# A PSUM ring for scores and PV products, with a new step order, in a sliding-window attention and gMLP kernel

## The chip, the cores and the metric

The kernel runs on one core of a Trainium2 chip. The metric is the device time in microseconds of one execution. The profile and its trace come from one execution; its span is about 1.7 us shorter than that execution's time. Runs have a state: fast, or slow when a run is over 1.5% above the fastest of the same kernel. Ratios use fast runs alone; medians are of all runs of a call.

Engines in the profile: PE is TensorE, PEld its weight loads, DVE is VectorE, ACT is ScalarE, POOL is GpSimd, SP issues most DMAs. An instruction is named by its source line: L447 is line 447 of that kernel's file, so the same step has another line number in an edited kernel.

## The reference

Eight batches of 576 rows. Attention has 8 heads of 64 columns with a causal window of 64, and the layer behind it is a gated MLP with a spatial product:

```python
scores = scale * np.matmul(q, k.transpose(0, 1, 3, 2))
mask = (rel >= 0) & (rel < 64)                       # rel = row - column
attn = softmax(np.where(mask, scores, -1e9))
x = (attn @ v), heads side by side                   # B, 576, 512
h = np.maximum(x @ w_in, 0.0)                        # 512 -> 1024
u, v = h[..., :512], h[..., 512:]
v_n = (v - mean(v)) / np.sqrt(var(v) + 1e-6)
v_s = einsum('ts,bsd->btd', w_spatial, v_n) + b_spatial
return (u * v_s) @ w_out
```

## The kernel before

The kernel is one list of about 1200 short words. Each word is a step, and the words are issued in the order of the list; each engine then works through its own instructions strictly in that order.

```python
    for word in ORDER.split():
        op, *args = word.split(".")
        OPS[op](*[int(a) if a.isdigit() else a for a in args])
```

A batch `b` passes through these steps (`s` is a pair of heads; s = 4 holds the last 64 rows of all heads):

- `l`, `lv` load q, k, v on SP; `c`, `cv`, `sh` cast and shift them, mostly on GpSimd; `T` and `to` transpose.
- `S` scores on TensorE, `E` exp on ScalarE, `M` mask on VectorE, `P` the product with V and with ones on TensorE, `n1` ln of the row sums, `n2` exp(-ln) and `x` the product, which is the normalised attention.
- `V`, `U` the two halves of w_in, `Q` the rest rows; `vo`, `ru` evacuate them; `bs`, `rs`, `ln` are the norm (`rs` is an ln and an exp on ScalarE); `G`, `g` the spatial product, `O`, `oc`, `st` the output.
- `H` are warming matmuls on zeros; they are meant to keep TensorE's clock up.

Scores and PV products each have a buffer of two PSUM banks, everything else shares four single banks:

```python
    def mm(name, shape=(128, 512), dtype=f32):
        return new(psp, list(shape), dtype, "mm", 4, name)
    def pe_S(b, s):
        sc = new(psp, [128, 2, 512], f32, "sc", 1, f"sc{b}_{s}")     # one buffer
        ...
    def pe_P(b, s):
        oz = new(psp, [128, 2, 512], f32, "oz", 1, f"oz{b}_{s}")     # one buffer
        ...
```

`table` loads a table set for ScalarE that serves all of its functions:

```python
    _need = {AF.Exp, AF.Ln, AF.Copy, AF.Identity, AF.Relu}
    _tbl_id = next(i for i, (_n, _f) in enumerate(_tables.items()) if _need <= _f)

    def k_table():
        nc.scalar.add_instruction(
            mybir.InstLoadActFuncSet(name=f"I-{nc.next_id()}", act_func_set_id=_tbl_id,
                                     ins=[], outs=[]))
```

Nothing in the program depends on `table`: no tile is written by it and none is read.

The softmax here doesn't subtract the row's maximum and nothing guards it: scores larger than these inputs give would overflow.

Of the kernel before, what the change touches and what calls it, by code (L numbers as in the profile page):

```python
# [14 lines left out]
S = 576  # L15
# [5 lines left out]
keep scratch l.0.k.0 H.4 id mask lv.0.1 maskr lv.0.0 l.0.q.0 table l.0.q.1 H.6 l.0.k.1 c.0.k.0.D  # L21
l.0.q.4 l.0.q.2 cv.0.0.P l.0.k.2 lv.0.2 c.0.q.0.P H.2 l.0.k.4 sh.0.0.1.P T.0.q.0 l.0.k.3 T.0.k.0
to.0.q.0.A c.0.q.1.P to.0.k.0.D lv.0.3 ones.1 lv.0.5 c.0.k.1.D S.0.0 c.0.q.4.P l.1.q.0 T.0.q.1 E.0.0
small H.2 lv.0.4 H.3 c.0.q.2.P to.0.q.1.A M.0.0 sh.0.0.0.P lv.0.7 T.0.k.1 T.0.q.2 c.0.k.2.D l.0.q.3
P.0.0 lv.1.0 c.0.k.4.P n1.0.0 to.0.k.1.D T.0.k.2 n2.0.0 lv.0.6 S.0.1 x.0.0 l.1.k.0 cv.0.1.P H.4
E.0.1 to.0.k.2.D l.1.k.1 sh.0.1.1.P to.0.q.2.A sh.0.1.0.P lv.0.8 M.0.1 S.0.2 lv.1.1 cv.0.2.P
c.0.k.3.D E.0.2 P.0.1 l.1.q.1 win.1 H.3 n1.0.1 l.1.k.2 c.0.q.3.D T.0.k.3 sh.0.2.1.P n2.0.1 lv.1.3
to.0.k.3.D T.0.q.3 lv.1.2 H.2 to.0.q.3.A win.0 M.0.2 T.0.q.4 l.1.q.2 T.0.k.4 x.0.1 S.0.3 cv.0.3.P
E.0.3 sh.0.2.0.P P.0.2 l.1.q.3 n1.0.2 sh.0.3.1.P M.0.3 H.3 n2.0.2 sh.0.3.0.P to.0.q.4.A x.0.2 ones.0
wsp to.0.k.4.D P.0.3 n1.0.3 S.0.4 V.0.1.0.3 n2.0.3 lv.1.8 V.0.2.0.3 cv.0.4.P E.0.4 x.0.3 sh.0.4.0.P  # L30
V.0.0.0.3 M.0.4 V.0.1.3.4 c.1.k.0.P V.0.2.3.4 vo.0.1.D V.0.0.3.4 vo.0.2.A P.0.4 c.1.k.1.P n1.0.4
U.0.1 c.1.q.0.P n2.0.4 vo.0.0.A x.0.4 lv.1.4 cv.1.0.P U.0.0 bs.0.2 ru.0.1 bs.0.1 Q.0 ru.0.0 T.1.k.0
U.0.2 vo.0.4.A to.1.k.0.D T.1.q.0 bs.0.4 l.1.q.4 c.1.q.1.P V.0.3.0.3 to.1.q.0.A sh.1.0.0.P T.1.k.1
ru.0.2 S.1.0 to.1.k.1.D sh.1.0.1.P V.0.3.3.4 E.1.0 W.0 vo.0.3.D U.0.3 l.1.k.3 wo.0.A M.1.0 lv.1.5
T.1.q.1 W.2 bs.0.3 l.1.k.4 cv.1.1.P to.1.q.1.A P.1.0 ru.0.3 bs.0.0 sh.1.1.0.P W.4 lv.1.7 wo.2.A
S.1.1 c.1.q.2.P wo.4.D rs.0 W.1 lv.1.6 c.1.k.2.P U.0.4 ln.0.3 wo.1.A l.2.k.0 wout W.3 ln.0.0 ru.0.4
l.2.q.0 E.1.1 T.1.k.2 ln.0.2 T.1.q.2 ln.0.1 lv.2.5 wo.3.D to.1.q.2.A ln.0.4 G.0.1 l.2.q.3 M.1.1
n1.1.0 G.0.0 l.2.k.1 cv.1.2.P to.1.k.2.D n2.1.0 sh.1.2.0.P x.1.0 G.0.3 sh.1.1.1.P g.0.0 lv.2.2
c.1.q.3.P g.0.1 S.1.2 G.0.2 c.1.q.4.P E.1.2 g.0.3 c.1.k.4.P P.1.1 sh.1.2.1.P g.0.2 l.2.k.4 n1.1.1
O.0.0 c.1.k.3.P M.1.2 lv.2.1 n2.1.1 cv.1.3.P T.1.q.3 G.0.4 oc.0.0.A x.1.1 lv.2.0 to.1.q.3.A T.1.k.3  # L40
cv.1.4.P P.1.2 lv.2.4 to.1.k.3.D c.2.k.0.P n1.1.2 T.1.k.4 lv.2.3 g.0.4 T.1.q.4 S.1.3 sh.1.3.0.P
to.1.k.4.D n2.1.2 O.0.1 l.2.q.1 c.2.q.0.P E.1.3 x.1.2 O.0.2 sh.1.3.1.P lv.2.6 to.1.q.4.A M.1.3
c.2.k.1.P oc.0.1.A l.2.q.2 T.2.k.0 S.1.4 oc.0.2.A to.2.k.0.D lv.2.7 P.1.3 E.1.4 sh.1.4.0.P l.2.k.2
O.0.3 n1.1.3 M.1.4 c.2.k.4.P l.3.k.1 n2.1.3 T.2.q.0 V.1.1.0.2 l.2.q.4 to.2.q.0.A cv.2.0.P V.1.1.2.3
x.1.3 lv.3.0 V.1.0.0.2 oc.0.3.A sh.2.0.1.P V.1.0.2.3 P.1.4 st.0.1 cv.2.2.P S.2.0 n1.1.4 l.2.k.3
V.1.1.3.4 E.2.0 c.2.q.1.P V.1.2.0.2 vo.1.1.D V.1.3.0.2 cv.2.1.P l.3.k.3 n2.1.4 V.1.3.2.3 M.2.0
V.1.0.3.4 sh.2.0.0.P l.3.k.0 T.2.k.1 vo.1.0.A V.1.3.3.4 x.1.4 V.1.2.2.3 lv.3.3 vo.1.3.D V.1.2.3.4
c.2.q.2.P P.2.0 vo.1.2.A to.2.k.1.D lv.2.8 c.2.q.3.P T.2.q.1 n1.2.0 T.2.q.2 bs.1.1 U.1.0 l.3.q.3
sh.2.2.1.P n2.2.0 st.0.0 bs.1.3 cv.2.3.P to.2.q.1.A U.1.1 ru.1.0 lv.3.6 sh.2.1.0.P x.2.0 to.2.q.2.A
S.2.1 sh.2.3.1.P bs.1.2 lv.3.1 Q.1 E.2.1 c.2.k.2.P bs.1.0 lv.3.4 c.2.q.4.P ru.1.1 U.1.2 M.2.1  # L50
vo.1.4.A l.3.q.0 sh.2.1.1.P U.1.4 oc.0.4.A lv.3.7 bs.1.4 T.2.k.2 ru.1.2 U.1.3 l.3.q.2 c.2.k.3.P
ru.1.4 to.2.k.2.D rs.1 st.0.3 T.2.k.3 ru.1.3 ln.1.2 S.2.2 ln.1.1 P.2.1 l.4.k.2 E.2.2 ln.1.0 ln.1.3
T.2.q.3 lv.3.2 ln.1.4 G.1.0 c.3.q.3.P n1.2.1 M.2.2 l.3.k.2 n2.2.1 sh.2.2.0.P l.3.q.4 G.1.3
to.2.q.3.A x.2.1 l.4.k.4 to.2.k.3.D c.3.k.0.P P.2.2 l.3.q.1 cv.2.4.P g.1.0 n1.2.2 T.2.k.4 T.2.q.4
S.2.3 sh.2.3.0.P g.1.3 lv.4.1 n2.2.2 G.1.1 st.0.2 to.2.k.4.D c.3.k.1.P E.2.3 x.2.2 sh.2.4.0.P
l.3.k.4 G.1.4 g.1.1 to.2.q.4.A cv.3.3.P lv.3.5 T.3.k.1 M.2.3 G.1.2 cv.3.0.P st.0.4 to.3.k.1.D
l.4.k.5 S.2.4 P.2.3 sh.3.3.0.P g.1.2 l.4.k.6 n1.2.3 O.1.0 g.1.4 c.3.q.2.P c.3.q.0.P O.1.2 oc.1.0.A
c.3.q.4.P n2.2.3 st.1.0 T.3.k.0 c.3.k.2.P O.1.1 oc.1.2.A to.3.k.0.D l.4.q.2 sh.3.0.1.P E.2.4 l.4.q.0
x.2.3 T.3.q.0 c.3.q.1.P V.2.1.0.4 lv.4.2 to.3.q.0.A M.2.4 sh.3.0.0.P l.4.k.7 S.3.0 vo.2.1.A lv.3.8
P.2.4 oc.1.1.A c.3.k.3.P O.1.3 n1.2.4 cv.3.1.P E.3.0 V.2.2.0.4 sh.3.3.1.P oc.1.3.A T.3.q.1 M.3.0  # L60
sh.3.1.1.P V.2.3.0.4 n2.2.4 vo.2.2.A x.2.4 V.2.0.0.4 sh.3.1.0.P vo.2.3.A bs.2.2 cv.3.2.P Q.2
vo.2.0.A bs.2.1 c.3.k.4.P to.3.q.1.A bs.2.0 P.3.0 sh.3.2.1.P l.5.k.6 vo.2.4.A T.3.q.2 l.5.k.5
oc.1.4.A cv.4.1.P U.2.1 bs.2.4 l.5.q.7 n1.3.0 sh.3.2.0.P st.1.3 to.3.q.2.A bs.2.3 S.3.1 c.4.k.1.P
ru.2.1 T.3.k.2 l.4.k.1 U.2.0 to.3.k.2.D E.3.1 st.1.2 l.5.q.4 U.2.2 n2.3.0 M.3.1 l.4.q.3 ru.2.0
T.3.q.3 l.4.k.3 x.3.0 U.2.4 rs.2 l.4.q.5 T.3.k.3 ru.2.2 S.3.2 ln.2.1 l.4.q.1 ln.2.2 to.3.q.3.A P.3.1
l.4.k.0 ln.2.3 ru.2.4 U.2.3 ln.2.0 E.3.2 st.1.4 ln.2.4 lv.4.0 R.4.k.1 G.2.0 n1.3.1 l.5.q.3
to.3.k.3.D n2.3.1 l.4.q.6 G.2.1 M.3.2 ru.2.3 lv.4.3 x.3.1 S.3.3 g.2.0 l.5.q.0 P.3.2 E.3.3 g.2.1
c.4.q.0.P l.5.k.4 T.3.k.4 T.3.q.4 to.3.k.4.D G.2.3 to.3.q.4.A M.3.3 l.5.k.7 n1.3.2 c.4.k.0.P st.1.1
n2.3.2 G.2.4 g.2.3 G.2.2 l.5.q.6 x.3.2 cv.4.2.P g.2.4 l.4.q.7 P.3.3 cv.4.0.P g.2.2 l.6.k.2 n1.3.3
S.3.4 cv.3.4.P R.4.q.0 O.2.1 n2.3.3 sh.3.4.0.P R.4.k.0 l.4.q.4 O.2.2 oc.2.1.A sh.4.0.0.P x.3.3  # L70
V.3.0.0.4 oc.2.2.A sh.4.0.1.P E.3.4 O.2.0 vo.3.0.A M.3.4 cv.4.3.P V.3.3.0.4 bs.3.0 sh.4.1.0.P S.4.0
P.3.4 E.4.0 O.2.3 sh.4.1.1.P n1.3.4 M.4.0 V.3.1.0.4 oc.2.0.A c.5.k.1.P n2.3.4 st.2.0 V.3.2.0.4
vo.3.3.A x.3.4 l.5.k.0 vo.3.1.A bs.3.3 lv.5.0 P.4.0 c.4.q.1.P oc.2.3.A l.5.k.3 Q.3 bs.3.1 vo.3.2.A
l.5.q.5 n1.4.0 bs.3.2 lv.5.4 S.4.1 vo.3.4.A lv.5.1 U.3.0 R.4.q.1 E.4.1 l.5.q.2 bs.3.4 l.6.k.0 U.3.1
oc.2.4.A cv.5.0.P l.5.q.1 n2.4.0 U.3.3 lv.4.4 rs.3 x.4.0 l.5.k.2 ru.3.0 U.3.4 st.2.1 M.4.1 ru.3.1
S.4.2 l.5.k.1 ln.3.2 P.4.1 ln.3.4 E.4.2 ln.3.0 U.3.2 ln.3.1 st.2.2 ln.3.3 ru.3.3 M.4.2 G.3.0 lv.5.3
ru.3.4 n1.4.1 l.6.k.3 n2.4.1 S.4.3 g.3.0 ru.3.2 c.5.q.0.P G.3.1 x.4.1 E.4.3 cv.4.4.P P.4.2 g.3.1
lv.6.4 n1.4.2 G.3.2 M.4.3 lv.5.2 n2.4.2 l.7.q.3 c.5.k.0.P G.3.3 x.4.2 st.2.3 lv.6.1 g.3.2 cv.5.4.P
P.4.3 l.7.q.5 g.3.3 cv.5.3.P st.2.4 n1.4.3 S.4.4 R.5.q.0 G.3.4 sh.4.4.0.P E.4.4 l.6.k.1 O.3.0
R.5.k.0 n2.4.3 c.5.q.1.P M.4.4 O.3.1 cv.5.1.P l.6.q.4 O.3.2 g.3.4 oc.3.1.A l.7.k.4 x.4.3 cv.5.2.P  # L80
lv.6.2 S.5.0 oc.3.2.A R.5.k.1 lv.6.0 sh.5.0.1.P P.4.4 oc.3.0.A R.5.q.1 V.4.0.0.4 E.5.0 sh.5.1.1.P
l.6.k.6 V.4.3.0.4 vo.4.0.A lv.6.3 sh.5.1.0.P n1.4.4 bs.4.0 V.4.2.0.4 l.6.k.7 n2.4.4 vo.4.3.A l.6.q.5
x.4.4 V.4.1.0.4 sh.5.4.0.P M.5.0 l.6.q.2 cv.6.4.P O.3.3 vo.4.1.A l.6.q.0 vo.4.2.A bs.4.1 sh.5.0.0.P
S.5.1 Q.4 l.6.q.1 bs.4.2 E.5.1 c.6.k.0.P bs.4.3 P.5.0 oc.3.3.A l.6.q.7 vo.4.4.A S.5.2 cv.6.1.P
l.6.q.3 oc.3.4.A bs.4.4 U.4.0 n1.5.0 U.4.1 M.5.1 n2.5.0 lv.7.4 rs.4 x.5.0 st.3.1 U.4.2 E.5.2 ln.4.1
l.7.q.1 ln.4.2 U.4.3 ru.4.2 M.5.2 st.3.4 ru.4.0 P.5.1 ln.4.4 ru.4.1 ln.4.3 st.3.2 S.5.3 ln.4.0
n1.5.1 l.6.q.6 U.4.4 n2.5.1 G.4.0 ru.4.3 l.6.k.5 x.5.1 E.5.3 c.6.q.0.P lv.7.2 G.4.3 g.4.0 st.3.0
ru.4.4 M.5.3 cv.6.0.P P.5.2 l.6.k.4 g.4.3 n1.5.2 G.4.1 st.3.3 sh.6.0.0.P n2.5.2 G.4.2 x.5.2 cv.6.3.P
g.4.1 G.4.4 g.4.2 S.5.4 g.4.4 P.5.3 E.5.4 R.6.k.0 O.4.0 n1.5.3 cv.7.2.P M.5.4 c.6.q.1.P n2.5.3 O.4.2
R.6.q.0 O.4.1 x.5.3 oc.4.2.A cv.6.2.P oc.4.0.A R.6.q.1 st.4.2 V.5.1.0.4 sh.6.1.1.P l.7.k.6 V.5.0.0.4  # L90
l.7.k.5 vo.5.1.A c.6.k.1.P l.7.q.6 bs.5.1 P.5.4 vo.5.0.A l.7.k.1 S.6.0 oc.4.1.A l.7.q.2 bs.5.0
# [23 lines left out]
def kernel(  # L115
# [13 lines left out]
    f32 = dt.float32  # L129
# [37 lines left out]
    G = {}  # L167
# [509 lines left out]
```

## Time and profile before

| | before |
|---|---|
| time, median of 3 runs | 220.54 us (218.71 to 222.54) |
| profiled run | 227.03 us, span 225.3 us |
| TensorE busy | 206.5 us, 92% |
| ScalarE busy | 156.7 us, 70% |
| table loads on ScalarE | 2 |

A row of the timeline is: start, duration, engine, line, operation, output<-input, count; the bracket is the idle time ahead of it and what ended it. Two rows of ScalarE's timeline show how the softmax of batch 0 runs in the kernel before: the exp follows the ln at once.

```profile
11.77 0.60 ACT L493 ACTIVATE ln<-oz 128x512 f32<-128x512 f32 x1 [1.49 <-PE oz L487]
12.39 0.63 ACT L500 ACTIVATE zi<-ln 128x512 f32<-128x512 f32 x1
```

ScalarE had been idle for 1.49 us before this ln, because P was not done.

### The profile page before, as it was taken

What the parts mean: (1) busy time and instruction counts of PE and PEld (TensorE: products, weight loads), DVE (VectorE), ACT (ScalarE), POOL (GpSimd) and SP (SyncE); (2) the same over time, 40 slices, a digit from 0 to 9 for tenths busy, and PEclk for the clock granted to TensorE, in tenths of its full rate; (3) what the DMA queues carried; (4) which work ended last, traced back from release to release, by engine and by line L of the source; (5) the groups of instructions that cost most, each with busy time, mean ns of one, the idle gap of its engine ahead of it and who ended that gap; (6) DMA issues with size and microseconds to landing.
All of it is one profiled execution on the core that took longest, in us unless ns stands there. A gap on an engine that the chain in (4) does not pass through costs nothing.

```text
span 225.3 us, 6646 instructions
## 1 busy us (share of the span) xinstructions
PE 206.5 (92%) x2726; PEld 110.3 (49%) x2726; DVE 154.9 (69%) x299; ACT 156.7 (70%) x291; POOL 116.3 (52%) x162
## 2 busy tenths in 40 slices
PE   7866699899999899999999999998599999999993
PEld 2443236555555455555555545554454555454450
DVE  3466638987699938896787887584665968665530
ACT  6467357858797489965995779659367489857623
POOL 2769915998916996099313993067839700000000
PEclk9999679999999999999999999999769999999999
DMA  5999999999999869997499999999970014000605
GB/s 170 251 262 242 223 243 174 271 185 256 283 271 213 227 163 249 220 175 150 116 201 245 207 181 184 201 278 248 257 184 3 0 49 145 24 0 3 207 22 192
DMA packets 77647, 40.43 MB, mean 179 GB/s; under 512 B 44272, under 2 KB 73008, under 8 KB 77616
## 3 DMA queue, kind: packets, MB, share of 16 engines
q1 hardware_dynamic: 75392, 37.76, 73.7%
q0 software_dynamic: 2224, 2.24, 6.1%
q8 instruction: 21, 0.34, 0.7%
q14 instruction: 10, 0.08, 0.2%
HBM read 32.79 MB, written 9.44 MB: 187 GB/s over the span
## 4 chain that ended last, share of the span: by engine, by line
PE 55%; ACT 11%; DMA 10%; SPq 10%; POOL 6%; DVE 4%; issue 2%; POOLq 0%
PE ps L603 14%; PE pv L522 10%; PE po L617 9%; PE pu L580 8%; DMA win<-in_moe_w_in_dram 4%; DMA fk<-in_k_dram 4%; PE oz L477 4%; SPq L304 4%; PE oz L487 3%; PE sc L415 3%; DMA vf<-in_v_dram 2%; ACT ob L624 2%; SPq L295 2%; DVE vn L571 2%; DVE e L463 2%
## 5 line engine op out<-in xcount | busy, mean ns | idle before, releaser
L603 PE MATMUL ps<-wspT,vn 128*128 128x512 f16 (+1 forms) x256 | 39.0, 286 | 0.9 <-DVE vn L571 0.8
L508 DVE TENSOR_TENSOR x<-oz,zi 128x512 f16<-128x512 f32 (+1 forms) x40 | 25.2, 630 | 19.8 <-ACT zi L500 19.7
L493 ACT ACTIVATE ln<-oz 128x512 f32<-128x512 f32 (+1 forms) x40 | 22.4, 561 | 22.9 <-PE oz L487 22.6
L447 ACT ACTIVATE e<-sc 128x1024 f16<-128x1024 f32 x32 | 32.7, 1022 | 6.7 <-PE sc L404 4.6
L522 PE MATMUL pv<-win,x 128*128 128x512 f16 x128 | 33.3, 403 | 1.9 <-DMA win<-in_moe_w_in_dram 1.9
L580 PE MATMUL pu<-x,win 128*128 128x512 f16 x128 | 32.4, 395 | 0.0
L463 DVE TENSOR_TENSOR e<-e,mask 128x1024 f16<-128x1024 f16 x32 | 26.2, 820 | 8.4 <-ACT e L447 8.3
L617 PE MATMUL po<-wout,g 128*128 128x512 f16 x128 | 31.2, 380 | 0.0
L553 DVE BATCH_NORM_STATS2 st<-vs 128x6 f32<-128x512 f16 (+1 forms) x40 | 27.0, 674 | 4.9 <-ACT vs L547 4.8
L547 ACT ACTIVATE vs<-pv 128x512 f16<-128x512 f32 (+1 forms) x36 | 21.2, 601 | 11.5 <-PE pv L522 10.0
L610 DVE TENSOR_TENSOR g<-ps,ru 128x512 f16<-128x512 f32 (+1 forms) x40 | 24.2, 630 | 7.1 <-PE ps L603 6.8
L624 ACT COPY ob<-po 128x512 f32<-128x512 f32 (+1 forms) x33 | 18.8, 587 | 12.8 <-PE po L617 12.4
L500 ACT ACTIVATE zi<-ln 128x512 f32<-128x512 f32 (+1 forms) x40 | 23.6, 590 | 0.9
L603 PEld LDWEIGHTS <-vn 128*128 128x128 f16 x256 | 16.7, 97 | 14.8 <-DVE vn L571 2.0
L593 ACT ACTIVATE ru<-pu 128x512 f32<-128x512 f32 (+1 forms) x40 | 20.9, 553 | 2.1 <-PE pu L580 2.0
L354 POOL COPY vs<-vn 64x512 f16<-64x512 f16 (+1 forms) x24 | 21.1, 885 | 1.3
L331 POOL CAST nq<-fq 128x1152 f16<-128x1152 f32 x8 | 9.9, 1237 | 22.2 <-DMA fq<-in_q_dram 14.7
L340 POOL CAST vn<-vf 128x512 f16<-128x512 f32 (+1 forms) x24 | 15.6, 657 | 10.4 <-DMA vf<-in_v_dram 10.3
L522 PEld LDWEIGHTS <-x 128*128 128x128 f16 x128 | 12.6, 102 | 16.6 <-issue 4.7
L352 POOL COPY vs<-vn 64x512 f16<-64x512 f16 (+1 forms) x24 | 20.4, 848 | 0.5
L580 PEld LDWEIGHTS <-win 128*128 128x128 f16 x128 | 11.7, 100 | 13.5 <-issue 2.7
L603 PE MATMUL ps<-wspT,vlast 65*128 65x512 f16 (+1 forms) x64 | 17.1, 288 | 0.0
(102 smaller groups left out, 350.9 us busy)
## 6 DMA issues: line engine op xcount, KB each, us to landing
out_dram<-ob SPq DMA_DIRECT2D x32, 256.0 KB, 3.7
vf<-in_v_dram SPq DMA_DIRECT2D x40, 128.0 KB, 5.4
fk<-in_k_dram SPq DMA_DIRECT2D x32, 144.0 KB, 5.2
fq<-in_q_dram SPq DMA_DIRECT2D x32, 144.0 KB, 5.5
fk<-in_k_dram SPq DMA_DIRECT2D x16, 256.0 KB, 5.9
fq<-in_q_dram SPq DMA_DIRECT2D x16, 256.0 KB, 5.1
vf<-in_v_dram SPq DMA_DIRECT2D x16, 256.0 KB, 5.8
win<-in_moe_w_in_dram POOLq DMA_DIRECT2D x2, 512.0 KB, 10.0
```

The source lines that it names most:

```text
L447: nc.scalar.activation(e2[:, :, :], sc[0][:, :, :], AF.Exp, bias=0.0, scale=0.125)
L463: nc.vector.tensor_tensor(e2[:, :, :], e2[:, :, :], m, ALU.min)
L493: nc.scalar.activation(lnz[:, 0:n], OZ[b, s][:, 1, 0:n], AF.Ln)
L500: nc.scalar.activation(zinv[:, 0:n], lnz[:, 0:n], AF.Exp, bias=0.0, scale=-1.0)
L508: nc.vector.tensor_tensor(x[:, 0:n], oz[:, 0, 0:n], zinv[:, 0:n], ALU.mult)
L522: nc.tensor.matmul(PV[b, j][0:jn, :], xcol(b, r, j), w_in_sb[:, r, 512:1024], start=(r == 0), stop=(r == 3))
L553: nc.vector.bn_stats(st6[0:jn, 0:6], VSB[b, j][0:jn, :])
L580: nc.tensor.matmul(pu[:, :], w_in_sb[:, r, 128 * m:128 * m + 128], X[b, r][:, :], start=(r == 0), stop=(r == 3))
L603: nc.tensor.matmul(o, VN[b, kk][0:kn, 128 * mm_:128 * mm_ + 128], w, start=(kk == 0), stop=(kk == 4))
L610: nc.vector.tensor_tensor(g[:, :], ps[:, 0:n], RU.pop((b, m))[:, 0:n], ALU.mult)
L617: nc.tensor.matmul(po[:, :], G[b, r][:, 128 * j:128 * j + 128], w_out_sb[:, r, :], start=(r == 0), stop=(r == 3))
L624: COPY[e](ob[p, :], po[p, :])
```

## The change

Its intent: with a ring of two two-bank buffers, shared by scores and PV products in turn, S no longer waits for the E of the step before and P no longer for the x of the step before; and a search over step orders, on a timing model that was calibrated anew, gives the order that makes use of it. The code part is small:

```diff
-        sc = new(psp, [128, 2, 512], f32, "sc", 1, f"sc{b}_{s}")
+        sc = new(psp, [128, 2, 512], f32, "att", 2, f"sc{b}_{s}")
...
     def pe_P(b, s):
-        oz = new(psp, [128, 2, 512], f32, "oz", 1, f"oz{b}_{s}")
+        if s < 4:
+            oz = new(psp, [128, 2, 512], f32, "att", 2, f"oz{b}_{s}")
+        else:
+            oz = mm(f"oz{b}_4", (128, 2, 256))
```

The order is replaced as a whole, by the same words in another sequence. Two lines of it (the rest is cut):

```diff
-keep scratch l.0.k.0 H.4 id mask lv.0.1 maskr lv.0.0 l.0.q.0 table l.0.q.1 H.6 l.0.k.1 c.0.k.0.D
...
+G.0.4 cv.1.2.P g.0.1 to.1.q.2.A G.0.0 c.1.k.2.P g.0.4 table M.1.1 l.2.q.1 c.1.q.3.P T.1.k.2 T.1.k.3
```

## The prediction

> **What bounds the kernel now.** I read the page first: busy shares, then the 40 slices.
>
> ```profile
> PE 206.5 (92%) x2726; PEld 110.3 (49%) x2726; DVE 154.9 (69%) x299; ACT 156.7 (70%) x291; POOL 116.3 (52%) x162
> ...
> PE   7866699899999899999999999998599999999993
> ...
> PEclk9999679999999999999999999999769999999999
> DMA  5999999999999869997499999999970014000605
> ```
>
> TensorE is busy nearly everywhere except in the first five slices (28 us) and in slices 29 to 31, and in both places its clock drops. DMA is full until about 168 us and then nearly idle. This profiled run was a slow one: its span is 225.3 us and its time 227.03, against a median of 220.54, so a usual run has a span of about 219 (6 us less), and I must not explain those 6 us away as gain.
>
> Next the totals by stage (columns: stretch, its length, then busy us of PE, PEld, DVE, ACT, POOL, then granted clock, DMA share, GB/s).
>
> ```profile
> 0.00:25.58 25.58, 17.18 (x221) 9.35 (x222) 12.77 (x31) 16.70 (x26) 17.94 (x35) 0.97 1.07 232
> 25.58:31.30 5.72, 5.72 (x23) 2.01 (x23) 3.15 (x2) 0.60 (x1) 3.54 (x6) 0.52 1.21 201
> ...
> 49.34:157.60 108.26, 105.02 (x1543) 58.19 (x1541) 83.77 (x158) 85.74 (x161) 66.29 (x87) 1.00 0.98 214
> 157.60:168.50 10.90, 8.52 (x132) 5.15 (x132) 7.26 (x17) 5.62 (x11) 6.14 (x6) 0.69 1.03 230
> 168.50:221.50 53.00, 52.90 (x622) 26.35 (x612) 32.61 (x65) 34.70 (x70) 9.97 (x12) 1.00 0.17 59
> ```
>
> I turn this into a loss account. In dense stretches of the timeline a group of four 512-column matmuls takes 0.866 us, five take 1.08, an S step 0.35 (batches 0 to 3) or 0.59, a P step 0.60, a transpose step 0.225, a Q step 0.89. Summed over the step order this is 184 us of TensorE work, plus 6 us of warming matmuls. After the first O step (49.3 us) 158 us of it remain, and TensorE ends at 221.5: 172 us for 158, a loss of 14. Of that 5.4 lie in 157.6 to 168.5 (a wait of 2.3 us and then half clock, most likely this run's own), 1.6 after it, and some 7 in 49 to 157. Before 49.3 only 26 us of real work were done: that is where 23 us went, and it is the chain of waits that shows why:
>
> ```profile
> 10.46 4.97 DMA vf<-in_v_dram
> ...
> 15.50 0.67 POOL vs L352
> 16.16 0.51 POOL vn L337
> 16.68 8.86 DMA win<-in_moe_w_in_dram
> ...
> 25.58 5.28 PE pv L522 x12
> ```
>
> The first V product waits for w_in, whose load GpSimd issues only after twelve casts and shifts; the last x of batch 0 was ready at 25.46, at the same moment. So the start has two chains of equal length, w_in and the softmax chain of batch 0.
>
> **What the Trainium skill says.** "PSUM — Partial Sum Buffer", section "Specifications (TRN2)": eight banks of 512 fp32 values per partition. The kernel's buffers agree: sc 2 banks, oz 2, four single ones, 8 in all; the ring takes 2 x 2 plus 4, again 8. "TensorE: Matmul & The Clock Gate", Part 1: an idle window of about 3.4 us halves the clock, a busy one restores it. The trace agrees: clock 0.52 in 25.58 to 31.30. "ScalarE: Activation LUTs", sections "What ACT_TABLE_LOAD costs" and "Table sets: the hidden batching unit": about 1283 ns per load, plus a drain; `exp_and_others` has exp but not ln, `natural_log_exp_and_others` both; and a compiler pass puts a load before every activation that needs one. The before kernel shows two loads:
>
> ```profile
> 0.80 1.28 ACT L238 ACT_TABLE_LOAD   x1 [0.80 <-PEq L661]
> ...
> 3.47 1.28 ACT L205 ACT_TABLE_LOAD   x1
> 7.34 0.58 ACT L382 COPY tr<-tp_0q 128x512 f16<-128x512 f16 x1 [2.59 <-PE tp_0q L372]
> ```
>
> The duration agrees; the drain does not show (the copy before the second load ended at 3.45). L205 is the kernel's own step "table", which names a set with exp, ln, copy and relu. L238 is a load that nobody wrote: it was put ahead of the mask copy, because "maskr" stands before "table". So an activation reached before "table" gets a load of the compiler's choosing.
>
> **The change part by part.** I counted the words of both orders: the same 1173 steps with the same engine letters. No instruction is removed or added by hand; each row's duration should stay.
>
> 1. The ring. S(s+1) no longer waits for E(s), nor P(s+1) for x(s); instead each takes the older of two pairs of banks, and P of step 4 goes to the single buffers. What single buffers cost before: the waits put down to it are (who waited for whom: us in total, times, longest)
>
> ```profile
> ACT ln L493 <- PE oz L487: 22.6, 19, 3.4
> ...
> ACT e L447 <- PE sc L404: 4.6, 5, 2.6
> ...
> PE oz L477 <- DVE x L508: 2.0, 2, 1.3
> ```
>
> The last is the direct one: 2.0 us, two times, both in the first 23 us. ScalarE's 22.6 us before ln and 4.6 before exp are idle time of an engine that is not the bound. The ring can also give more overlap of E, M, P, n1, n2, x where TensorE waited on a mask step (0.41 us at 54.7, 1.11 at 77.6). I give the ring 1 to 3 us.
>
> 2. The order at the start. In the new order eleven, not twelve, casts and shifts precede w_in's load on GpSimd, and their inputs come earlier. Counting queue positions at 0.55 us each and about 4.5 us to landing, it should be issued near 14.5 instead of 16.7: w_in 2 us earlier.
>
> 3. Order and stores later. On the SP queue a store that waits holds the loads behind it: waits put down to L630 sum to 53.7 us in 12 times. One, from 102.3 to 109.0, is the dent of slices 18 and 19 of DMA. In the new order the comparable store of batch 2 stands even earlier (63 loads behind it, against 54), others later; no clear gain. Of the 8 us lost after 49 us in a usual run I let a better order recover 3.
>
> 4. "table" moves from before the first real activation to the middle of batch 1, after E.1.1. This is the part I weigh most. Until then ScalarE's order is exp, exp, ln, exp, ln, exp and so on. If the pass loads the exp set first and for each ln a set without exp, I count 14 loads: the mask copy, n1/n2 of steps 0 and 1 (4), n1.2, n2.2, n1.4, n2.3 (4), the two halves of rs.0, n1 and n2 of batch 1 step 0, and "table" itself. That is 12 more than now: 12 x 1.283 = 15.4 us of ScalarE, all before some 53 us.
>
> How much of it reaches the path? A load ahead of an ln can hide under the wait for P; one ahead of n2's exp cannot. Walking the steps with durations of the before profile (E 1.0, mask 0.7, P 0.6, ln 0.6, exp 0.63, to 0.58): with the loads, n1.0.0 falls at 14.5, n2.0.1 ends near 23, E.0.3 near 26, and from there four loads (5.1) and 2.8 us of activations lead to x.0.3 at about 34.7, against 25.5 now. Then V.0, U.0, the two loads of rs.0, and G.0 starts near 47.5 instead of 43.2; then T.1.k.3 needs a PSUM buffer that the evacuation of T.1.q.2 frees only behind two more loads and E.1.1, near 53. With 161 us of work left there, TensorE is some 7 us later than the before trace at the same point (161 left falls at 46).
>
> Sum with the loads: 220.5 + 7 (it contains the 2 us of w_in, which is then hidden) - 3 (ring and order later) = 224.5. Without them: 220.5 - 1.5 (start; the softmax chain of batch 0 binds then) - 3 = 216.
>
> **The rivals.** (a) The loads come and bind: 224.5. For it: the unwritten load at L238, and the fact that the kernel's author bothers to name one set. Against it: the search may know the loads. (b) The pass picks the common set at the first ln, or the loads hide: one or two more loads, 216. Nothing in the before trace shows how it picks. (c) The loads come but the lost time is regained, because DMA runs on while TensorE is late, and later waits for data (157 to 161 us) shrink: about 220. For it: DMA is full to 168 us and the chain runs through loads at 119 and 155. Against it: loads stand behind stores on SP, and these come later when TensorE is late. (d) The ring couples S to x two steps back, a longer chain than to E: S.0.4 would wait for x.0.1; 1 to 2 us worse, early only.
>
> **Range and chances.** I give the loads 0.8 (a and c together), and within them 224.5 and 220 some 2 to 1; (b) 0.2. An order that was searched would hardly have been kept had it been much worse on a chip, which pulls me below 224. The middle is 222.0 us, the range 214.5 to 228.5. Faster by over 2% is below 216.1: 0.16. Slower is above 224.95: 0.32. Within 2%: 0.52.
>
> **What would show it.** ACT_TABLE_LOAD in the groups: 14 and some 18 us for step 4 right, 2 or 3 for wrong. In the timeline, w_in issued near 14.5; x.0.3 near 35 (right) or 25 (wrong); the first 512-column G near 47. The 54 us before the end should stay dense as now. If DMA ends well before 160, my 3 us for the later order were too few. A prediction of 222 falls if loads are there and the time is still under 216: then the start was hidden under something that I took for following it.

## The result, and the profile after

| | before | after |
|---|---|---|
| time, median of 4 runs each | 221.54 us (218.71 to 223.41) | 228.66 us (226.99 to 229.41) |
| profiled span | 225.3 us | 227.7 us |
| mean granted TensorE clock in that run | 0.970 | 0.948 |
| TensorE busy | 206.5 us | 205.2 us |
| ScalarE busy, instructions | 156.7 us, 291 | 172.0 us, 303 |

The ratio is 1.0401, with a 95% interval of 1.0279 to 1.0523. Ratios here are the mean time of one kernel's fast runs over that of the other's fast runs of the same rounds, so they are not quite the ratio of the medians. The changed kernel is slower by 4%.

The slices of the changed kernel:

```profile
PE   7494575959899999999999999999999999999993
...
PEclk9957578897999999999999999999999999999999
```

The holes have moved. From slice 12 on TensorE is full and its clock is at 9 or more; the dip that the kernel before has in slices 28 to 30 is gone (its profile is of a slow run, so the dip may be that run's own). But the first eleven slices (63 us) are worse than before: TensorE at 4 to 5 tenths in five of them, and a clock under 9 in seven (3 to 8 and 10), where the kernel before had two such slices there, 5 and 6.

ScalarE's extra 15.3 us are twelve instructions. These are the table loads among the groups of the changed kernel (line, engine, operation, count, then busy us and mean ns of one, then idle time before):

```profile
L496 ACT ACT_TABLE_LOAD x5 | 6.4, 1283 | 0.1
L503 ACT ACT_TABLE_LOAD x5 | 6.4, 1283 | 0.1
...
L238 ACT ACT_TABLE_LOAD x1 | 1.3, 1283 | 0.8 <-PEq L664 0.8
L563 ACT ACT_TABLE_LOAD x1 | 1.3, 1283 | 0.0
L564 ACT ACT_TABLE_LOAD x1 | 1.3, 1283 | 0.0
L205 ACT ACT_TABLE_LOAD x1 | 1.3, 1283 | 0.0
```

L496 is n1, L503 is n2, L563 and L564 are the ln and the exp of `rs`. Fourteen loads, one at each change between exp and ln, until `table` (L205). ScalarE's timeline of batch 0, where before ln and exp stood next to each other:

```profile
13.93 1.02 ACT L447 ACTIVATE e<-sc 128x1024 f16<-128x1024 f32 x1 [0.94 <-PE sc L404]
14.97 1.28 ACT L496 ACT_TABLE_LOAD   x1
16.27 0.60 ACT L496 ACTIVATE ln<-oz 128x512 f32<-128x512 f32 x1
16.88 1.28 ACT L503 ACT_TABLE_LOAD   x1
18.18 0.63 ACT L503 ACTIVATE zi<-ln 128x512 f32<-128x512 f32 x1
...
20.82 1.28 ACT L496 ACT_TABLE_LOAD   x1
22.11 0.60 ACT L496 ACTIVATE ln<-oz 128x512 f32<-128x512 f32 x1
```

A load waits for no tile, so an empty bracket ahead of it does not tell whether it pushes the ln behind it. That is told by when P, for which the ln waits, was done on TensorE. P of step 0 ends at 15.20, so the load at 14.97 hides for only 0.2 of its 1.28 us; P of step 1 ends at 17.15, long before the load at 20.82, which does not hide at all. The load ahead of the third ln (28.50) does: the chain of waits passes there through matmuls of P that end at 29.81, and not through the load. The chain of waits of the changed kernel (start, us, what) runs through the same rows on to the first V product; a part of it:

```profile
32.35 0.04 ACT L496
32.38 1.26 issue
33.64 0.87 ACT ln L496 x2
34.51 0.02 issue
34.53 1.28 ACT L503
...
36.48 0.70 DVE x L511
37.19 0.05 issue
37.23 2.41 PE pv L525 x7
39.64 0.43 PE tp_0k L372 x4
40.07 1.61 PE pu L583 x4
```

Here a table load appears as "ACT L503" with no tile, or as "issue". Seven V products wait for the x at 36.48 and then take 2.41 us, where seven at full clock take 1.5 (7 x 0.2165 us, a fourth of a dense group of 0.866): TensorE has been waiting, and its clock is down. With the transposes and the U step behind them they take 4.45 us, where 2.6 would do (1.52, 0.22 and 0.87).

### The profile page after: what moved, and what is told of

It is laid out like the page before. It is cut to its first block, busy times and chain, and to the rows that moved or that the text cites. A ratio compares the mean times of both kernels' runs of the same rounds, so it can differ in the third digit from the quotient of the medians.

```text
span 227.7 us, 6658 instructions
## 1 busy us (share of the span) xinstructions
PE 205.2 (90%) x2726; PEld 109.6 (48%) x2726; DVE 151.4 (66%) x299; ACT 172.0 (76%) x303; POOL 113.0 (50%) x162
## 4 chain that ended last, share of the span: by engine, by line
PE 73%; ACT 15%; DVE 5%; issue 3%; DMA 2%; SPq 1%; POOL 0%; ACTq 0%
PE ps L606 14%; PE po L620 13%; PE pv L525 12%; PE pu L583 10%; PE oz L480 4%; PE oz L490 3%; PE pv L537 3%; PE sc L415 3%; PE sc L404 3%; ACT e L447 3%; ACT L503 2%; DMA fq<-in_q_dram 2%; DVE e L463 2%; ACT L496 2%; ACT zi L503 2%
## 5 line engine op out<-in xcount | busy, mean ns | idle before, releaser
L606 PE MATMUL ps<-wspT,vn 128*128 128x512 f16 (+1 forms) x256 | 39.6, 289 | 0.1
L525 PE MATMUL pv<-win,x 128*128 128x512 f16 x128 | 32.5, 387 | 3.8 <-DVE x L511 3.8
L496 ACT ACTIVATE ln<-oz 128x512 f32<-128x512 f32 (+1 forms) x40 | 21.8, 553 | 12.6 <-PE oz L490 12.2
L596 ACT ACTIVATE ru<-pu 128x512 f32<-128x512 f32 (+1 forms) x40 | 21.4, 552 | 8.0 <-PE pu L588 5.3
L503 ACT ACTIVATE zi<-ln 128x512 f32<-128x512 f32 (+1 forms) x40 | 23.4, 590 | 0.6
L354 POOL COPY vs<-vn 64x512 f16<-64x512 f16 (+1 forms) x24 | 18.9, 792 | 1.4
L525 PEld LDWEIGHTS <-x 128*128 128x128 f16 x128 | 11.4, 99 | 16.9 <-DVE x L511 5.2
L352 POOL COPY vs<-vn 64x512 f16<-64x512 f16 (+1 forms) x24 | 18.8, 782 | 0.7
L620 PEld LDWEIGHTS <-g 128*128 128x128 f16 x128 | 11.6, 98 | 12.9 <-DVE g L613 0.5
L583 PEld LDWEIGHTS <-win 128*128 128x128 f16 x128 | 11.5, 99 | 12.2 <-issue 1.1
```

The costliest lines, as they stand in the source:

```text
L496: nc.scalar.activation(lnz[:, 0:n], OZ[b, s][:, 1, 0:n], AF.Ln)
L503: nc.scalar.activation(zinv[:, 0:n], lnz[:, 0:n], AF.Exp, bias=0.0, scale=-1.0)
L525: nc.tensor.matmul(PV[b, j][0:jn, :], xcol(b, r, j), w_in_sb[:, r, 512:1024], start=(r == 0), stop=(r == 3))
L583: nc.tensor.matmul(pu[:, :], w_in_sb[:, r, 128 * m:128 * m + 128], X[b, r][:, :], start=(r == 0), stop=(r == 3))
L596: nc.scalar.activation(RU[b, m][:, 0:n], pu[:, 0:n], AF.Relu)
L606: nc.tensor.matmul(o, VN[b, kk][0:kn, 128 * mm_:128 * mm_ + 128], w, start=(kk == 0), stop=(kk == 4))
```

## The experiments

The theories. **L**: the table loads cause the loss, by taking ScalarE's time in the early chain. **R**: the ring causes it, since S now waits for the x of two steps back (the trace does show one such wait, 3.7 us ahead of S of step 4 of batch 0). **O**: the new order is bad in some other way. All edits are to the order of words unless shown. Calls ran on different chips, and the kernel before differs between calls (median of its fast runs 219.6 to 221.5 us), so differences under some 2 us are read within one call only.

### First call: which part

**a_table_early.** The changed kernel with one word moved.

```diff
-... mask l.0.k.1 maskr l.0.q.4 ...
+... mask l.0.k.1 maskr table l.0.q.4 ...
-... c.1.k.2.P g.0.4 table M.1.1 ...
+... c.1.k.2.P g.0.4 M.1.1 ...
```

> The changed kernel with one word moved: the step "table" back to just behind the mask copy at the start, as the kernel before has it. Theory L (the table loads cause the loss): 2 loads instead of 14 on ScalarE, x.0.3 near 25 us instead of 37, and a time of about 214 us (211 to 218), so faster than the kernel before by some 3%. Theory R (the ring, which makes S wait for the x of two steps back, causes it) and theory O (the searched order causes it): 226 to 229 us as in the changed kernel, since neither is touched.

Measured: 216.44 us (four runs within 0.24 us), ratio to the kernel before 0.9849 (0.9758 to 0.9939). One word is worth 12 us, and the loss is gone. R and O are out as causes of the slowdown, since both the ring and all other words are unchanged. This kernel is also the right partner for reading the changed kernel's trace: it differs in one word, and both profiles are of fast runs. Totals by stage, cut at the first O step of batch 0 and at the end of TensorE's work; first the changed kernel, then this one (columns as in the prediction's table of stages):

```profile
0.00:63.48 63.48, 45.33 (x491) 24.55 (x492) 30.55 (x64) 46.64 (x65) 40.72 (x73) 0.81 0.98 214
63.48:223.90 160.42, 159.82 (x2237) 85.07 (x2236) 120.87 (x236) 124.78 (x238) 72.28 (x90) 1.00 0.73 164
```

```profile
0.00:48.94 48.94, 37.96 (x491) 21.27 (x492) 31.20 (x64) 31.10 (x53) 35.40 (x61) 1.00 1.08 232
48.94:211.00 162.06, 159.90 (x2237) 84.78 (x2236) 121.99 (x236) 124.89 (x238) 80.79 (x101) 1.00 0.79 176
```

The same 491 matmuls precede the first O step in both. They end 14.5 us later in the changed kernel, and 12 more table loads last 12 x 1.283 = 15.4 us. The two numbers are close, but this is not a proof that nothing hid. The chain of waits of the changed kernel passes through eleven of the loads (14.1 us) and through matmuls at a lower clock, and a_table_early has waits of its own in which a part of this goes: 1.67 us for P ahead of the third ln, 1.44 us of U for the first half of w_in. And 1.2 us stand ahead of the first extra load. The exp of step 1 begins at 13.93 in the changed kernel (shown above); here it begins at

```profile
12.76 1.02 ACT L447 ACTIVATE e<-sc 128x1024 f16<-128x1024 f32 x1 [0.17 <-PE sc L404]
```

mostly because TensorE's clock from 8 to 14 us was 0.73 in the changed kernel's profile and 1.00 in this one. Behind the first O step the stage is 1.6 us shorter in the changed kernel; that is all that is regained. Look also at the clock, 0.81 against 1.00, and at TensorE's busy time, 45.3 against 38.0 us for the same matmuls.

**b_table_late.** The kernel before, with its `table` where the changed kernel has it.

```diff
-... lv.0.0 l.0.q.0 table l.0.q.1 H.6 ...
+... lv.0.0 l.0.q.0 l.0.q.1 H.6 ...
-... S.1.2 c.1.q.4.P E.1.2 g.0.3 ...
+... S.1.2 c.1.q.4.P table E.1.2 g.0.3 ...
```

> The kernel before with only the step "table" moved to where the changed kernel has it, just ahead of E of batch 1, step 2. Counted by the rule that fitted the changed kernel this makes 16 loads (14 more than now, 18 us of ScalarE). Theory L: 10 to 15 us slower than the kernel before, 231 to 236 us. Theories R and O: no change beyond noise, 219 to 223 us.

Measured: 233.35 us, ratio 1.0622 (1.0515 to 1.0729). The trace has 16 loads, as counted. Without any ring and without the new order the loads cost 6%. Theory L holds in both orders.

**b_ring_only.** The old order and its early `table`, with the ring (the code part of the change alone).

> The kernel before with its own order and its early "table", but with the two-bank ring in place of the separate sc and oz buffers and P of step 4 in a single buffer. Theory L: the ring is worth little either way in an order not made for it, 218 to 223 us. Theory R: most of the 8 us of loss is here, 226 us or more. Theory O: 218 to 223 us.

Measured: 221.08 us, ratio 1.0071 (0.9986 to 1.0156). The ring in an order not made for it shows no gain; the range allows a loss of up to 1.6%.

**a_table_mid.** The changed kernel with `table` moved up to just ahead of `rs.0`; its trace has 10 loads.

> The changed kernel with "table" moved up only to just ahead of rs.0: counted, 10 loads instead of 14, so the 8 extra loads of batch 0 stay and the 4 of rs.0 and of batch 1 step 0 go. Theory L with the loss in proportion to the loads on the path: about two thirds of the way between 214 and 228.7, that is 222 to 225 us. If only the loads of batch 0 matter (the later ones hide behind dense TensorE work): still 227 to 229. If only the later ones matter: near 215. Theories R and O: 226 to 229.

Measured: 226.23 us, ratio 1.0261 (1.0135 to 1.0386). The 8 extra loads of batch 0 cost 9.8 us against a_table_early (9.1 us by the ratios; one of the four runs is slow), the other 4 some 2.4 to 3 more (against the 228.66 us of other rounds). This is a little more than the two thirds that I expected (222 to 225): the loads of batch 0 count most. That the later four cost less than their 5.1 us is not shown, since the ranges of the two ratios overlap.

### Second call: which loads, and does the place matter

All of these keep `table` early and add explicit loads of the same common set, so that the results stay right and only ScalarE's time changes.

**a_loads_ln.** Six extra loads, each ahead of an ln.

```diff
-... n1.0.0 ...      (and n1.0.1, n1.0.2, n1.0.4, rs.0, n1.1.0)
+... table n1.0.0 ...
```

> The changed kernel with "table" early (216.4 us), plus 6 extra loads of the same common set, each put just ahead of an ln of the early part (n1 of steps 0, 1, 2, 4 of batch 0, the ln of rs.0, n1 of batch 1 step 0): half of the 12 extra loads of the changed kernel, at the places where I predicted that a load hides under the wait for P. If that holds: 217 to 219 us. If a load costs the same wherever it stands in this chain: half of the 12 us, about 222.

**a_loads_exp.** The other six, each ahead of an exp that follows an ln.

```diff
-... n2.0.0 ...      (and n2.0.1, n2.0.2, n2.0.3, n2.1.0)
+... table n2.0.0 ...
     def rs(b):
+        if b == 0: k_table()      # between the ln and the exp
```

> The same with the other 6 loads: each just ahead of an exp that follows an ln (n2 of steps 0, 1, 2, 3 of batch 0, the exp of rs.0, n2 of batch 1 step 0), where I predicted that nothing hides them. If that holds: 224 to 227 us. If all places cost alike: about 222.

Measured: 220.88 us for the six ahead of ln, ratio 0.9939 (0.9866 to 1.0012), and 221.98 us for the six ahead of exp, ratio 1.0004 (0.9934 to 1.0073). They differ by 1.1 us on the same chip, with overlapping ranges, where I expected at least 5. So my rule, that a load ahead of an ln hides and one ahead of an exp does not, is wrong as a rule. What six loads cost is less certain: by medians 4.4 and 5.5 us more than a_table_early, which ran on another chip (near the half that equal places would give), but by the ratios to the kernel before 2.0 and 3.4 us. The profiles keep a rest of the rule. The first O step comes 4.1 us later than in a_table_early with the loads ahead of ln, and 7.0 us later with those ahead of exp, but 1.5 us of the 7.0 stand ahead of the first of its loads. The trace of a_loads_ln shows where loads hid. These are the first four of its ln steps, with the loads:

```profile
13.54 1.28 ACT L206 ACT_TABLE_LOAD   x1
14.83 0.60 ACT L497 ACTIVATE ln<-oz 128x512 f32<-128x512 f32 x1
...
18.11 1.28 ACT L206 ACT_TABLE_LOAD   x1
19.40 0.60 ACT L497 ACTIVATE ln<-oz 128x512 f32<-128x512 f32 x1
...
23.73 1.28 ACT L206 ACT_TABLE_LOAD   x1
25.03 0.60 ACT L497 ACTIVATE ln<-oz 128x512 f32<-128x512 f32 x1
...
26.30 1.28 ACT L206 ACT_TABLE_LOAD   x1
27.60 0.87 ACT L497 ACTIVATE ln<-oz 128x256 f32<-128x256 f32 x2
```

and the first three of a_table_early, without loads:

```profile
14.59 0.60 ACT L496 ACTIVATE ln<-oz 128x512 f32<-128x512 f32 x1 [0.81 <-PE oz L490]
...
17.73 0.63 ACT L496 ACTIVATE ln<-oz 128x512 f32<-128x512 f32 x1
...
23.75 0.60 ACT L496 ACTIVATE ln<-oz 128x512 f32<-128x512 f32 x1 [1.67 <-PE oz L490]
```

The first load hides for most of its length: 14.83 against 14.59, because ScalarE had 0.81 us of idle time there (and the exp of step 1 began 0.26 us earlier in this run). The second does not hide: 19.40 against 17.73, because no idle time stands ahead of that ln; P had been done since 15.5. The third hides wholly: the delay falls from 1.67 to 1.28 us, because the ln had 1.67 us to wait for P anyway. The fourth adds its length again. So a load ahead of an ln hid where the ln had to wait for P in the order that ran, and nowhere else; the idle time that I had seen ahead of ln (1.49 us) belongs to the old order. At the fourth of these ln steps (24.91 us in a_table_early) the four loads make it 2.7 us later, of 5.1. In the changed kernel, where loads ahead of exp stand between them, it comes 8.7 us later (33.64) with seven loads of 9.0 us; but some 1.8 us of the 8.7 are TensorE's lower clock (see a_warm).

**a_loads_later.** Twelve extra loads in the middle, each ahead of an output copy (`oc`) of batches 2, 3 and 4.

> The changed kernel with "table" early, plus 12 extra loads, each just ahead of an output copy of batches 2, 3 and 4: the same 15.4 us of ScalarE time as in the changed kernel, but in the dense middle. If it is the chain of batch 0 and 1 that turns loads into time: 216 to 219 us. If ScalarE time as such is what costs (ScalarE has become the bound): 226 to 229 us.

Measured: 235.89 us, ratio 1.0547 (1.0436 to 1.0659); the profiled run was slow, the two fast runs took 235.22 and 232.48. I was wrong on both sides: these 15.4 us do not hide, and the kernel is slower than either theory had it. By the ratios they cost 15.3 us against a_table_early (1.0547 / 0.9849), which is their whole length; by the mean of the two fast runs, on another chip, 17.4. ScalarE's timeline shows a reason:

```profile
101.82 1.28 ACT L205 ACT_TABLE_LOAD   x1
103.12 0.58 ACT L627 COPY ob<-po 128x512 f32<-128x512 f32 x1
103.72 1.28 ACT L205 ACT_TABLE_LOAD   x1
105.02 0.58 ACT L627 COPY ob<-po 128x512 f32<-128x512 f32 x1
```

An output copy frees one of the four single PSUM banks. In the new order three or four of them stand close together, and each now comes 1.3 us later. TensorE is then held up more than in a_table_early, where the first of these waits is 1.3 us and the second is missing (who waited for whom: us in total, times, longest):

```profile
PE ps L606 <- DVE vn L574: 8.3, 6, 3.4
PE pv L525 <- ACT ob L627: 4.9, 5, 2.1
```

As this trace is of a slow run, it is no measure of the size; that these waits for `ob` are new is what I take from it.

**a_order_only.** The new order with an early `table` but with the separate sc and oz buffers. The order is impossible as it stands (a P would write a buffer whose x is issued after it), so steps were moved down until it was possible, 24 of them by more than three words.

> The new order with "table" early but without the ring: separate sc and oz buffers as before, and the 24 steps that this makes impossible in their place (a P ahead of the x that frees its buffer, and what depends on it) moved down behind it. If the ring is what makes the new order 2 to 3% faster than the kernel before: back to 219 to 222 us. If the order alone does it: 216 to 218 us.

Measured: 251.32 us, ratio 1.1287 (1.1183 to 1.1391), far outside what I expected either way. In its trace, of a slow run, TensorE waits 9.3 us for x ahead of P and 11.6 us for E ahead of S; a_table_early has neither wait. This says that the new order, as it stands, cannot do without the ring. It does not say what the best order without a ring would be, because moving steps down is a crude repair.

### Third to fifth call: spread loads, the clock, a better kernel, idle time

**a_loads_spread.** Twelve extra loads in the middle again, each ahead of an n1 of batches 2, 3 and 4.

> The changed kernel with "table" early, plus 12 extra loads in the middle again (batches 2, 3, 4), but each just ahead of an ln of a softmax step (n1) instead of ahead of an output copy; so they do not come in groups of three or four. ScalarE sits idle ahead of ln for 13.8 us in 12 places of the kernel with the early table. If what counts is whether ScalarE was waiting there anyway, much of the 15.4 us hides: 218 to 224 us. If ScalarE time in the middle costs its full length wherever it is put: 232 us or more, as with the output copies (235.9).

Measured: 226.68 us, ratio 1.0274 (1.0201 to 1.0348). Spread out they cost 4.3% against a_table_early (1.0274 / 0.9849), some 9 to 10 us: less than ahead of the output copies, above what I expected, and 0.8 us a load. So in the middle, too, most of a load turns into time, although ScalarE, in a_table_early, is busy for only 77% of the time behind the first O step (124.9 of 162.1 us).

**a_warm.** The changed kernel with its 14 loads, plus 18 warming matmuls in TensorE's waits (`H.6` ahead of `S.0.4`, `V.0.3.0.3` and `V.0.3.3.4`).

> The changed kernel with its late "table" and all its 14 loads, plus three times six warming matmuls in the waits of TensorE that the loads make (ahead of S of step 4 and ahead of the first and the fourth group of V of batch 0). In the changed kernel TensorE is busy 205.2 us against 197.9 with the early table, for the same 2726 instructions, because the clock falls to half in these waits. If the slow clock is a part of the loss of its own: 224 to 227 us. If TensorE only waits for ScalarE there, so that a faster clock gains nothing: 228 to 230 us.

Measured: 227.79 us, ratio 1.0345 (1.0278 to 1.0412). The clock over the first 60 us rises from 0.80 to 0.91, and the time falls by 0.5 to 0.9 us (by medians, or by ratios of 1.0401 and 1.0345), which is within noise. I took this to say that the slow clock is a small part of the loss. It does not say so, because the warming stands in the way itself. The chain of waits of this run passes through six of the added matmuls, ahead of the V products:

```profile
34.44 1.03 DVE x L512 x2
35.47 0.04 issue
35.51 2.65 PE warm L639 x6
```

The x is ready 2.0 us earlier than in the changed kernel (34.44 against 36.48; 1.3 of this was there before the first added matmul), and 2.65 us of warming then take it back. What the lower clock costs can be read from the chain of the changed kernel alone: 1.1 us ahead of its first extra load, 0.7 us in S of steps 4 and 3 with the warming between them (1.97 us against 1.24 in this run), and 1.85 us in the V, transpose and U steps shown above (4.45 against 2.6). That is 3.7 us of matmul time on the path of one profiled run. In every kept trace with the late `table` the clock falls to 5 or 6 tenths in one or more of the first ten slices; in those of a_table_early, a_loads_start and a_loads_idle it stays at 9. But a_best (6) and a_loads_spread (7) have one such slice early as well, with no extra load there. How much of the 12 us the lower clock carries is not settled by a run.

**a_best.** The changed kernel with `table` ahead of the mask copy, and the first half of w_in loaded right behind the second.

```diff
-... mask l.0.k.1 maskr l.0.q.4 ...
+... mask l.0.k.1 table maskr l.0.q.4 ...
-... win.1 ones.0 ...
+... win.1 win.0 ones.0 ...
```

> An attempt to beat both kernels: the changed kernel with "table" ahead of the mask copy (one load in all) and the load of the first half of w_in issued right behind that of the second half, because in the run with the early table the first U waits 1.4 us for it. Expected 214.5 to 216 us against 216.4 with the early table alone; if w_in delays the other loads by as much as it gains, the same 216.4.

Measured: 215.45 us over six runs, ratio 0.9782 (0.9718 to 0.9846). It beats both kernels. The trace has one load instead of two, and the 1.4 us wait of U for w_in is gone from its list of waits; against a_table_early the gain is about 1 us, which two calls on two chips do not separate from noise.

**a_loads_start.** Three more loads written right behind the early `table`, in idle time.

> The changed kernel with "table" early, plus 3 more loads right behind it, in the 4.31 us in which ScalarE has nothing at all to do before the first evacuation of a transpose (5.2 to 9.5 us of its trace). 3 x 1.283 = 3.85 us fit. If a load costs nothing where the whole chain is waiting for DMA: 216 to 217 us. If every load costs about 1 us wherever it stands: 219 to 220.

Measured: 215.66 us, ratio 0.9726 (0.9649 to 0.9803). This run tells nothing on its question: its trace has 2 loads in all. The four loads that stood directly one behind another appear as one, so it was a_table_early once more, and shows the scatter between calls (0.8 us).

**a_loads_idle.** The mend: two more loads, each kept apart by a copy of one column.

```diff
-... maskr table l.0.q.4 ...
+... maskr table tiny table tiny table l.0.q.4 ...
```

> Mend of the run with 3 more loads at the start: its trace shows that the loads written one behind another were merged into one, so it was the kernel with the early "table" again (215.7 us against 216.4). Now 2 more loads, each kept apart from the one before by a copy of a single column, about 3.0 us together, inside the 4.1 us in which ScalarE has nothing to do before the first evacuation of a transpose. If a load is free where ScalarE has no work in hand: 215.5 to 217 us. If a load costs about 1 us wherever it stands: 217.5 to 219.

Measured: 214.91 us, ratio 0.9706 (0.9624 to 0.9787). The loads are there:

```profile
3.93 1.28 ACT L205 ACT_TABLE_LOAD   x1
5.23 0.19 ACT L212 COPY tiny<-scratch 128x1 f16<-128x1 f16 x1
5.44 1.28 ACT L205 ACT_TABLE_LOAD   x1
6.73 0.20 ACT L212 COPY tiny<-scratch 128x1 f16<-128x1 f16 x1
6.95 1.28 ACT L205 ACT_TABLE_LOAD   x1
9.66 0.58 ACT L387 COPY tr<-tp_1q 128x512 f16<-128x512 f16 x1 [1.43 <-PE tp_1q L377]
```

and they cost nothing: ScalarE still waits 1.43 us after them for the first transposes. A load was free where ScalarE had no work in hand, and cost up to its whole length where it had.

## Why the prediction was right or wrong

- **Step 4, which loads there would be: right.** Fourteen loads were predicted from the order of words alone and the trace has fourteen, at the places named. It rested on one row of the trace before, a load that nobody had written. Rival (b), that the common set would be chosen at the first ln, is out.
- **Step 4, how much reaches the path: this is the step that failed, by its size.** With the loads it gave 224.5 us and without them 216, so 8.5 us for the loads; measured are 228.66 and 216.44, so 12.2. What came short is the walk of the chain to the first G:

  | station | predicted | measured | late by |
  |---|---|---|---|
  | start of n1.0.0 | 14.5 | 16.27 | 1.8 |
  | end of n2.0.1 | 23 | 24.65 | 1.7 |
  | end of E.0.3 | 26 | 28.47 | 2.5 |
  | end of x.0.3 | 34.7 | 37.2 | 2.5 |
  | start of G | 47.5 | 53.28 | 5.8 |

  The largest term is TensorE's clock. The walk took "durations of the before profile", which are those of full clock. In the trace the matmuls on the chain take 3.7 us more: 1.1 ahead of n1.0.0, 0.7 ahead of E.0.3, and 1.85 between x.0.3 and G (worked out under a_warm). The hiding under the wait for P is a small term: the walk let only the load ahead of n1.0.0 hide (its 14.5 is where a_table_early, without that load, has the ln: 14.59), which accounts for at most 0.7 us, and from E.0.3 to x.0.3, where it counted all four loads, its 8.7 us were measured as 8.7. The last 1.4 us lie between x.0.3 and G as well: behind the loads of rs.0 the chain still holds an exp, an evacuation of U and three copies of the transposed W_spatial (49.78 to 52.78), which the walk does not name. This division is read from one trace; no run tests it, since a_warm does not separate the clock.
- **Step 1, the ring gives 1 to 3 us.** Alone it shows no gain (221.08 us). In the new order it cannot be taken away without a loss (251.32 us, with a crude repair). So it is what the new order stands on, and no gain of its own.
- **Step 2, w_in issued near 14.5: right** (15.02 in the trace), and worth nothing in the changed kernel, where x of step 3 came some 13 us later than w_in landed. Without the loads it is the other half of w_in that U waits for (1.4 us in a_table_early), which the step did not see.
- **Step 3, together with the ring and the start: the sum came out.** Without the loads I gave 216; a_table_early took 216.44. That the parts (1.5 us at the start, 3 later) are right as well is not shown: the only stage table of the kernel before is of a slow run. And against the kernel before of its own call (fast runs 219.6 us) the gain is 3.2 us, not 4.5, so some of the match is luck.
- **Rival (c)**, that the lost time is regained later, holds for 1.6 us only.
- **Rival (d)** was seen: S of step 4 waits 3.7 us for x in the changed kernel, 1.2 us with the early `table`. Most of that wait is itself made by the loads.
- **The middle and the range.** Rival (a), 224.5, was the one that came, and still 4 us too low. The middle of 222.0 came from mixing in (b) and (c), and from the thought that a searched order would hardly be kept if it were much worse; the measured 228.66 lies just outside the range of 214.5 to 228.5. That thought had no row of the profile behind it. Two smaller misreadings moved nothing: the dip late in the kernel before lies in slices 28 to 30, not 29 to 31, and the 53.7 us of L630 are its waits for output copies alone (with its other waits some 65).

## What to carry to other kernels

A step without inputs and outputs can still have an order: a search that moves steps by their data dependencies moves a state change such as a table load to where it does harm, and no check of results sees it, so pin such steps, or make every later step that relies on them depend on them. Idle share is not slack: an engine that was busy 73% of the span turned 0.3 to 1.3 us of each inserted load of 1.28 us into lost time, by the place (ratios of a_loads_ln and a_loads_later), and only time in which it had no work in hand took the loads for nothing. When you ask whether a cost hides, look for the idle time in the order that will run, not in the one that did. And when you walk a chain that will have new waits in it, do not give its matmuls the durations of a dense stretch: here seven V products took 2.41 us behind a wait, and 1.5 would have been their dense time.

## What the Trainium skill lacked or had wrong

- "ScalarE: Activation LUTs", section "Table sets: the hidden batching unit", gives one load for an ln followed by an exp, because one set has both. In this build the loads that were put in do not keep to that set: the changed kernel got a load at each change, 14 in all with the one named by hand, which came last.
- The same page, section "What ACT_TABLE_LOAD costs", gives about 1283 ns and a drain of about 1380 ns more per switch. The 1283 ns agree in every trace; the drain does not show. From the end of E at 14.95 us to the start of the ln at 16.27 us, with a load between them, pass 1.32 us.
- No page says that loads of one set written directly behind each other can end as one: four written in a_loads_start became one in the trace, while thirteen with activations between them (a_loads_later) stayed thirteen.
- "TensorE: Matmul & The Clock Gate", Part 1, puts the half clock behind an idle window of about 3.4 us. The prediction took the trace to agree, but only the half clock does: in the kernel before it was 0.52 from 25.58 to 31.30, and the wait just ahead of that lasted 1.9 us. That a busy stretch restores the clock agrees: in the changed kernel it is 0.81 in the 63 us in which TensorE has its waits, and 1.00 afterwards.
